# Transposes issued ahead of the loads two pairs on, and MoE pieces moved in front of the later first blocks, in an attention and feed-forward kernel

## The chip, the cores and the metric

The kernel runs on one core of one Trainium2 chip. The metric is the device time of one execution in microseconds (us). The engines of the core work side by side, each through its own queue of instructions in program order: PE (TensorE, matmuls), PEld (its weight loads), ACT (ScalarE), DVE (VectorE), POOL (GpSimd) and SP (SyncE, here only an issuer of DMAs).

## What is computed

Eight batches with eight heads each, 576 positions and head width 64. The attention has a decay: with `cum = cumsum(log(clip(f)))`, the scores are `q k^T / 8 + cum_i - cum_j`, masked to the causal half, softmaxed and multiplied by `v`. The heads of a position side by side make a row of 512 numbers, 4608 rows in all, and these go through a feed-forward layer, called MoE in the code:

```python
h = x @ w_in                          # 4608x512 by 512x2048
g = h * (1.0 / (1.0 + np.exp(-h)))
out = g @ w_out                       # 2048x512, float32
```

## The kernel before, in words

**The attention.** Each batch has a first block of 128 positions (all heads together, `turn0`, `scores0`, `out0`, `back0`) and the rest of its positions, done by pairs of heads: 4 pairs per batch, 32 pairs `n`. A pair takes this way. `load_qk(n)` (L144) issues four DMAs of 96 KB on SP for q and k in float32. `cast_qk(n)` (L371) has POOL write them as bf16 into a tile `qkb`, with a slice of a tails tile that `load_tails(b)` (L157) brings once per batch. `transposes(n)` (L400) is one DMA on SP, a DMA transpose from `qkb` into a tile `qkT` (L404). `scores(n, c)` (L425) for c = 0, 1, 2 multiplies on PE from `qkT` into PSUM, and ACT takes the exponential into `u`. `attend(n)` (L465) multiplies by the values, `back(m)` (L506) turns the results of two pairs and puts them into the rows `x` of the feed-forward layer.

**The buffers.** `qkT` has 3 buffers, which the first blocks use too, so that `transposes(n)` waits until `scores(n-3, 2)` has read the oldest; `qkb` has 4, the float32 stages 4, the output tiles `osb` 5. PSUM has two kinds: `psc`, 2 tiles for scores, and `pbig`, 4 tiles for all else (`hp`, `po`, `dn`, `tx`).

**The feed-forward layer.** The rows are cut into groups: group 0 is the first blocks of batches 0 to 3, group 1 those of 4 and 5, group 2 those of 6 and 7, then one group for the rest of each batch. A piece is either one `m1_chunk` (L528: four matmuls `hp`, then tanh on ACT and a product on DVE into `gt`) or one `m2_part` (L562: four matmuls `po` of width 512; after the fourth part of a tile ACT copies it to `osb`, and a store is kept in a list that SP issues later). A group's pieces can be placed only once it is in `ready`, and parts of the second product only once `open2` is set.

**The order.** It is written out by hand: every engine runs its instructions in the order in which the program emits them (L54). `fill(us)` (L641) emits pieces until their planned PE time, 4·(width/2.4 + 2.5) ns each, has used up `us` microseconds; it stops early if no piece can be placed. So the numbers in `fill` decide how many pieces stand at a place of the PE queue. `two_more(b, ...)` (L740) does the first blocks b and b+1 with small fills between; it stands twice, for 4 and 5, and for 6 and 7. After it comes the loop over m (L801), two pairs per pass: `scores`, `prepare(n)` (L772), a `slot` of pieces, and so on, with `attend` of both pairs at the end of a pass. `prepare(n)` issues what later pairs need: the loads of pair n+4, cast and transpose of pair n+2, tails and values of the next batch. `slot` also emits, after its pieces, the stores that were waiting before it.

Of the kernel before, what the change touches and what calls it, by code (L numbers as in the profile page):

```python
# [18 lines left out]
def kernel(  # L19
# [25 lines left out]
    NU = B * NP  # L45
# [95 lines left out]
    def head(p, i):  # L141
        return p // 2 * 4 + 2 * i + p % 2

    def load_qk(n):  # L144
        b, p = divmod(n, NP)
        ts = []
        for name, src in (("qf", q), ("kf", k)):
            t = stage.tile([P, NR, 2, D], FP32, name=name, tag=name, bufs=4)
            for i in range(2):
                nc.sync.dma_start(  # L150
                    out=t[:, :, i, :],
                    in_=src[b, head(p, i), P:SM, :].rearrange("(c p) d -> p c d", p=P),
                )
            ts.append(t)
        qst[n] = tuple(ts)

    def load_tails(b):  # L157
        t = stage.tile([P, H, D], FP32, name="qktf", tag="qktf", bufs=2)
        for i, src in enumerate((q, k)):
            nc.sync.dma_start(  # L160
                out=t[i * ST : (i + 1) * ST, :, :],
                in_=src[b, :, SM:S, :].rearrange("h s d -> s h d"),
            )
        tst[b] = t

    def load_v(b, c):
        if c == 0:
            vst[b] = []
        t = vfs[c]
        r = slice(0, P) if c < NR else slice(ST, P)  # L170
        nc.sync.dma_start(
            out=t[r, :, 0:D],
            in_=v[b, :, P + c * P : min(S, P + (c + 1) * P), :].rearrange("h p d -> p h d"),
        )
        vst[b].append(t)
# [195 lines left out]
    def cast_qk(n):  # L371
        b, p = divmod(n, NP)
        t2 = conv.tile([P, NX, 2 * D], BF16, name="qkb", tag="qkb")
        for i, t in enumerate(qst.pop(n)):
            c0 = i * (NR + 1)
            nc.gpsimd.tensor_copy(  # L376
                out=t2[:, c0 : c0 + NR, :].rearrange("p c x -> p (c x)"),
                in_=t[:, :, :, :].rearrange("p c h d -> p (c h d)"),
            )
        nc.gpsimd.tensor_copy(  # L380
            out=t2[:, NR, :].rearrange("s (i d) -> s i d", i=2),
            in_=tst[b].rearrange("s (u i w) d -> s u w i d", u=2, w=2)[:, p // 2, p % 2, :, :],
        )
        qbf[n] = t2

    def convert_v(b, c):
        vbf[b] = vps[b % 2]
        r = slice(0, P) if c < NR else slice(ST, P)
        n = r.stop - r.start
        nc.gpsimd.tensor_tensor(  # L390
            out=vbf[b][r, c, :, :],
            in0=vst[b][c][r, :, :],
            in1=w_bf[r, c + 1, b * H : (b + 1) * H, None].to_broadcast([n, H, D + 1]),
            op=ALU.mult,
        )
# [4 lines left out]
    def transposes(n):  # L400
        src = qbf.pop(n)
        t = qktp.tile([P, NX, P], BF16, name="qkT", tag="qkT")
        qkT[n] = t[:, :, :].rearrange("p x c -> p (x c)")
        nc.sync.dma_start_transpose(  # L404
            out=t[:, :, :], in_=src[:, :, :].rearrange("p x c -> p (x c)")
        )
# [200 lines left out]
    def step():  # L607

        a, c = at["m1"], at["m2"]
        can1 = a < len(M1) and M1[a][0] in ready  # L610
        g1 = M1[a][0] if a < len(M1) else NG
        g2 = M2[c][0] if c < len(M2) else NG
        if can1 and M1[a][1] == 0 and g1 > g2 + 1:
            can1 = False
        can2 = open2["w"] and c < len(M2) and g2 < g1
        if not can1 and not can2:
            return None
        if can1 and can2:
            f1 = M1[a][1] / NFC
            f2 = (c - sum(M2_OF[:g2])) / M2_OF[g2]  # L620
            want = 3 - at["last"] if abs(f1 - f2) < 0.15 else (1 if f1 < f2 else 2)
            if want == at["last"] and at["row"] >= 2 and abs(f1 - f2) < 0.25:
                want = 3 - want
            can1 = want == 1
        kind = 1 if can1 else 2
        at["row"] = at["row"] + 1 if kind == at["last"] else 1
        at["last"] = kind
        if can1:
            m1_chunk(*M1[a])
            at["m1"] += 1  # L630
            return 4 * (GW[g1] / 2.4 + 2.5)
        m2_part(*M2[c])
        at["m2"] += 1
        return 4 * (DM / 2.4 + 2.5)
# [6 lines left out]
    def fill(us_, first=0, least=0):  # L641
        if first:
            at["last"], at["row"] = 3 - first, 2
        at["left"] += us_ * 1000
        while at["left"] > 0 or least > 0:
            t = step()
            if t is None:
                at["left"] = 0.0
                return False
            at["left"] -= t  # L650
            least -= 1
        return True
# [76 lines left out]
    load_qk(2)  # L729
    load_v(0, 2)  # L730
    load_v(0, 3)
    for n in range(2):
        cast_qk(n)
        transposes(n)
    load_qk(3)
    load_tails(1)
    for c in range(NM):
        convert_v(0, c)
# [1 line left out]
    def two_more(b, banned):  # L740
        for x in range(2):
            turn0(b + x, 0)
            turn0(b + x, 1)
            fill(0.6, 0, 1)
        for x in range(2):
            if banned:
                scores0(b + x, ban0(b + x))
            else:
                scores0(b + x)
                mask0(b + x)  # L750
            fill(0.6 if x == 0 else 2.0, 2, 1 if x == 0 else 2)
        out0(b)
        fill(0.6, 0, 1)
        out0(b + 1)
        fill(0.8, 0, 2)
        back0(b, on_act)
        fill(0.6, 0, 1)
        back0(b + 1, on_act)
        fill(0.6, 2, 1)

    fill(4.0)
    two_more(4, True)
    ready.add(1)
    fill(6.0)
    open2["w"] = True
    fill(3.0, 2)
    two_more(6, False)
    ready.add(2)

# [2 lines left out]
    def prepare(n):  # L772

        b, p = divmod(n, NP)
        if n + 4 < NU:
            load_qk(n + 4)
        if n + 2 < NU:
            cast_qk(n + 2)
            transposes(n + 2)
        if p == 0 and b > 0 and b + 1 < B:  # L780
            load_tails(b + 1)
        if p == 1 and b + 1 < B:
            for c in range(NM):
                load_v(b + 1, c)
        if p >= 2 and b + 1 < B:
            for c in range(2 * (p - 2), 2 * (p - 1)):
                convert_v(b + 1, c)
# [13 lines left out]
    for m in range(NQ):  # L801
        n = 2 * m
        piece = 1.3 if m < 2 else 2.4
        scores(n, 0)
        scores(n, 1)
        prepare(n)
        slot(piece, 2)
        if m > 0:
            back(m - 1)
            if m % 2 == 0:  # L810
                b = m // 2 - 1
                pending.append([1, [REST_OF[b]] + ([TAILS_OF[b][0]] if b == NM - 1 else [])])
        scores(n, 2)
        scores(n + 1, 0)
        prepare(n + 1)
        slot(piece, 2)
        scores(n + 1, 1)
        scores(n + 1, 2)
        slot(piece, 2)
        attend(n)  # L820
        attend(n + 1)
        slot(min(3.5, max(0.8, behind() - LAG)) if m > 1 else 0.8, 1)
# [38 lines left out]
```

The softmax here doesn't subtract the row's maximum and nothing guards it: scores larger than these inputs give would overflow.

## Time and profile before

| | |
|---|---|
| time before, median of 13 runs | 360.06 us (358.74 to 362.7) |
| the profiled execution's own time | 359.35 us |
| its span in the profile | 357.6 us |
| PE busy | 342.6 us, 96% of the span |
| ACT busy | 219.3 us, 61% |
| DVE busy | 184.2 us, 52% |
| POOL busy | 103.1 us, 29% |
| moved by DMA | 47.92 MB, mean 134 GB/s |
| DMA transposes `qkT` on SP | 32, median 3.2 us from issue to landing |
| q and k loads on SP | 128 of 96 KB, medians 3.2 and 3.1 us to landing |

The profile is one execution. In a timeline, a row is a start, a length, an engine, a line of the kernel, the tiles (written <- read), a count, and in brackets the idle time before it and what ended that. In a list of waits a row names who waited for whom, the total, the number of times and the longest. The rows of a window view give the busy time of each engine in a stretch, then the clock that PE was granted (1.00 is full speed), the DMA share and rate. The time lies 1.75 us above the span, before and behind what the profile covers.

### The profile page before, as it was taken

What the parts mean: (1) busy time and instruction counts of PE and PEld (TensorE: products, weight loads), DVE (VectorE), ACT (ScalarE), POOL (GpSimd) and SP (SyncE); (2) the same over time, 40 slices, a digit from 0 to 9 for tenths busy, and PEclk for the clock granted to TensorE, in tenths of its full rate; (3) what the DMA queues carried; (4) which work ended last, traced back from release to release, by engine and by line L of the source; (5) the groups of instructions that cost most, each with busy time, mean ns of one, the idle gap of its engine ahead of it and who ended that gap; (6) DMA issues with size and microseconds to landing.
All of it is one profiled execution on the core that took longest, in us unless ns stands there. A gap on an engine that the chain in (4) does not pass through costs nothing.

```text
span 357.6 us, 9042 instructions
## 1 busy us (share of the span) xinstructions
PE 342.6 (96%) x3647; PEld 205.1 (57%) x3647; DVE 184.2 (52%) x408; ACT 219.3 (61%) x400; POOL 103.1 (29%) x183
## 2 busy tenths in 40 slices
PE   7999997779999999999999999999999999999995
PEld 3644554556756656656566565765656655555564
DVE  4565743435566655556554563456645553435340
ACT  5656646657586776866857567576776744444341
POOL 6975246263171351072072053116100000000000
PEclk9999999989999999999999999999999999999999
DMA  8999979899996966987596495498520001001012
GB/s 158 222 206 212 208 158 178 200 208 193 174 216 148 211 136 124 162 172 156 125 199 151 105 215 113 119 174 187 83 55 31 31 5 55 29 36 55 31 60 59
DMA packets 139001, 47.92 MB, mean 134 GB/s; under 512 B 128016, under 2 KB 134416, under 8 KB 138960
## 3 DMA queue, kind: packets, MB, share of 16 engines
q1 hardware_dynamic: 132272, 40.93, 55.8%
q0 software_dynamic: 6528, 6.29, 10.7%
q8 instruction: 28, 0.46, 0.6%
q10 hardware_dynamic: 160, 0.13, 0.1%
q14 instruction: 13, 0.11, 0.1%
HBM read 36.85 MB, written 9.44 MB: 129 GB/s over the span
## 4 chain that ended last, share of the span: by engine, by line
PE 75%; DMA 11%; SPq 5%; ACT 4%; issue 2%; POOL 1%; DVE 1%; ACTq 0%; POOLq 0%
PE po L580 32%; PE hp L535 28%; PE sc L436 6%; DMA vf<-in_v_dram 5%; PE dn L481 4%; DMA w_out_bf<-in_moe_w_out_dram 3%; SPq L150 3%; PE dn L490 2%; DMA qkT<-qkb 2%; ACT u L440 2%; PE tx L511 2%; DMA qkb<-in_q_dram 1%; SPq L160 1%; DVE gt L544 1%; ACT th L543 1%
## 5 line engine op out<-in xcount | busy, mean ns | idle before, releaser
L544 DVE SCALAR_TENSOR_TENSOR gt<-th,hp 128x384 bf16<-128x384 bf16 (+2 forms) x208 | 106.4, 522 | 83.7 <-ACT th L543 80.0
L580 PE MATMUL po<-w_out_bf,gt 128*128 128x512 bf16 (+1 forms) x592 | 147.7, 376 | 0.0
L543 ACT ACTIVATE th<-hp 128x384 bf16<-128x384 f32 (+2 forms) x208 | 96.0, 476 | 84.0 <-PE hp L535 79.1
L535 PE MATMUL hp<-x,w_in_bf 128*128 128x384 bf16 (+2 forms) x704 | 130.5, 322 | 1.1 <-DVE gt L544 0.8
L535 PEld LDWEIGHTS <-w_in_bf 128*128 128x128 bf16 x832 | 79.1, 98 | 56.5 <-issue 3.1
L440 ACT ACTIVATE u<-sc 128x1024 bf16<-128x1024 f32 (+1 forms) x96 | 74.5, 816 | 22.2 <-PE sc L436 22.0
L580 PEld LDWEIGHTS <-gt 128*128 128x128 bf16 x592 | 54.5, 98 | 48.8 <-issue 3.5
L390 POOL TENSOR_TENSOR vp<-vf,w_bf 128x520 bf16<-128x520 f32 (+1 forms) x32 | 34.3, 1074 | 58.0 <-DMA vf<-in_v_dram 41.7
L445 DVE TENSOR_TENSOR u<-u,tri 128x768 bf16<-128x768 bf16 x32 | 18.6, 582 | 30.8 <-ACT u L440 30.7
L436 PE MATMUL sc<-qkT 64*128 64x128 bf16 (+1 forms) x640 | 26.9, 208 | 5.3 <-DMA qkT<-qkb 4.6
L590 ACT ACTIVATE osb<-po 128x512 f32<-128x512 f32 (+1 forms) x37 | 22.0, 595 | 15.0 <-PE po L580 15.0
L376 POOL CAST qkb<-qf 128x384 bf16<-128x384 f32 x32 | 16.1, 504 | 46.5 <-DMA qf<-in_q_dram 46.0
L436 PEld LDWEIGHTS <-qkT 64*128 64x128 bf16 x640 | 18.4, 95 | 14.9 <-DMA qkT<-qkb 6.1
L459 DVE TENSOR_TENSOR ut<-ut,trit 128x128 bf16<-128x128 bf16 x32 | 9.2, 288 | 31.6 <-ACT ut L452 31.3
L452 ACT ACTIVATE ut<-sc 128x640 bf16<-128x640 f32 x32 | 22.9, 716 | 0.0
L481 PEld LDWEIGHTS <-u 128*128 128x128 bf16 x576 | 20.9, 97 | 3.3 <-issue 1.1
L481 PE MATMUL dn<-vp,u 128*128 128x65 bf16 x384 | 21.8, 193 | 0.0
L481 PE MATMUL dn<-v,u 128*128 128x65 bf16 x192 | 19.8, 193 | 0.9 <-DVE gt L544 0.8
L499 DVE TENSOR_TENSOR xr<-dn,rec 128x448 bf16<-128x448 f32 x32 | 20.0, 624 | 1.1
L376 POOL CAST qkb<-kf 128x384 bf16<-128x384 f32 x32 | 17.0, 533 | 9.7 <-DMA kf<-in_k_dram 9.6
L535 PE MATMUL hp<-xt,w_in_bf 128*128 128x256 bf16 x128 | 17.7, 273 | 0.0
L436 PE MATMUL sc<-qkT,kT 64*128 64x64 bf16 (+1 forms) x128 | 16.0, 258 | 0.0
(65 smaller groups left out, 202.3 us busy)
## 6 DMA issues: line engine op xcount, KB each, us to landing
vf<-in_v_dram SPq DMA_DIRECT2D x32, 256.0 KB, 4.8
out_dram<-osb SPq DMA_DIRECT2D x32, 256.0 KB, 2.2
qf<-in_q_dram SPq DMA_DIRECT2D x64, 96.0 KB, 3.2
kf<-in_k_dram SPq DMA_DIRECT2D x64, 96.0 KB, 3.1
w_in_bf<-in_moe_w_in_dram POOLq DMA_DIRECT2D x4, 512.0 KB, 8.9
w_out_bf<-in_moe_w_out_dram POOLq DMA_DIRECT2D x4, 512.0 KB, 11.0
qkb<-in_q_dram POOLq DMA_DIRECT2D x8, 128.0 KB, 5.9
qkb<-in_k_dram POOLq DMA_DIRECT2D x8, 128.0 KB, 6.6
```

The lines of the kernel that those rows point to most:

```text
L376: nc.gpsimd.tensor_copy(out=t2[:, c0 : c0 + NR, :].rearrange("p c x -> p (c x)"), in_=t[:, :, :, :].rearrange("p c h d -> p (c h d)"),)
L390: nc.gpsimd.tensor_tensor(out=vbf[b][r, c, :, :], in0=vst[b][c][r, :, :], in1=w_bf[r, c + 1, b * H : (b + 1) * H, None].to_broadcast([n, H ...
L436: nc.tensor.matmul(sc[:, i, o : o + q1 - q0], lhsT=kt, rhs=t[r, q0:q1], start=True, stop=True)
L440: nc.scalar.activation(out=u[:, :, c * SM : c * SM + w], in_=sc[:, :, 0:w], func=ACT.Exp, scale=scale)
L452: nc.scalar.activation(out=ut[:, :, 0:3:2, :].rearrange("p k i t -> p i k t"), in_=sc[:, :, T0 : T0 + (NM + 1) * ST].rearrange("p i (k t) ...
L481: nc.tensor.matmul(dn[:, i * NR + c - 1, :], lhsT=u[:, i, o : o + P], rhs=vals(kb, i), start=(kb == 0), stop=(kb == c),)
L499: nc.vector.tensor_tensor(out=xq[:, :, p % 2, :], in0=dn[:, :, 0:D], in1=rec[:, :, None].to_broadcast([P, NGR, D]), op=ALU.mult,)
L535: nc.tensor.matmul(hp[:, :], lhsT=w_in_bf[:, cc, fc * P : (fc + 1) * P], rhs=xg(g)[:, cc, :], start=(cc == 0), stop=(cc == NCC - 1),)
L543: nc.scalar.activation(out=th[:, :], in_=hp[:, :], func=ACT.Tanh, scale=0.5)
L544: nc.vector.scalar_tensor_tensor(out=gt[:, fc, :], in0=th[:, :], scalar=1.0, in1=hp[:, :], op0=ALU.add, op1=ALU.mult,)
L580: nc.tensor.matmul(po[:, :], lhsT=gt[:, fc, tb * P : (tb + 1) * P], rhs=w_out_bf[:, fc, m0:m1], start=(fc == 0), stop=(fc == NFC - 1),)
L590: nc.scalar.activation(out=osb[:, :], in_=po[:, :], func=ACT.Copy, scale=0.5)
```

## The change

Two kinds of edits. The DMA transposes are put ahead of loads in the order of SP: in `prepare`, the cast and transpose of pair n+2 now come before the loads of pair n+4, and in the run-up the loads of pair 3 come before the casts and transposes of pairs 0 and 1. And three arguments of `fill` change, in front of the first blocks 4 and 5 and of 6 and 7. The work itself is the same: no instruction is added or removed. POOL's order does not change.

```diff
     load_v(0, 3)
+    load_qk(3)
     for n in range(2):
         cast_qk(n)
         transposes(n)
-    load_qk(3)
     load_tails(1)
...
-    fill(4.0)
+    fill(6.0)
     two_more(4, True)
     ready.add(1)
-    fill(6.0)
+    fill(5.0)
     open2["w"] = True
-    fill(3.0, 2)
+    fill(6.0, 2)
     two_more(6, False)
     ready.add(2)
...
     def prepare(n):
 
         b, p = divmod(n, NP)
-        if n + 4 < NU:
-            load_qk(n + 4)
         if n + 2 < NU:
             cast_qk(n + 2)
             transposes(n + 2)
+        if n + 4 < NU:
+            load_qk(n + 4)
```

Compared instruction by instruction, the two PE queues hold the same 3647 matmuls. In front of `turn0(4)` stand seven `hp` pieces of width 512 instead of five. Between `two_more(4)` and `turn0(6)` stand twelve `hp` pieces of width 256 and seven `po` pieces, instead of two `hp` of 512, seven of 256 and three `po`. The pieces that are placed earlier are missing from the fills of later passes of the loop; from the last `back` on the two queues are alike again. On SP each transpose from pair 2 on stands ahead of one `load_qk` that it stood behind, and three stores instead of two stand ahead of the transpose of pair 3.

## The prediction

> **What bounds the kernel now.** I read the page's busy shares first, then the waits of PE, then PE's timeline around each wait, and last SP's timeline in the same stretch. PE is busy for 342.6 of 357.6 us, so the time can fall only where PE stands still or runs slowly. The list of PE's waits is short:
>
> ```profile
> PE sc L436 <- DMA qkT<-qkb: 4.6, 2, 3.1
> PE tp L271 <- DMA qkb<-in_q_dram: 1.7, 3, 1.0
> PE hp L535 <- DVE gt L544: 0.8, 1, 0.8
> PE dn L481 <- DVE gt L544: 0.8, 1, 0.8
> PE sc L436 <- ACT u L440: 0.5, 1, 0.5
> ```
>
> The timeline of PE places them (start, length, operation, count, idle before):
>
> ```profile
> 26.25 0.64 PE L271 MATMUL tp<-sel,qkb 128*64 128x64 bf16 x16 [0.31 <-DMA qkb<-in_q_dram]
> 27.13 0.64 PE L271 MATMUL tp<-sel,qkb 128*64 128x64 bf16 x16 [0.24 <-DMA qkb<-in_k_dram]
> ...
> 58.51 0.40 PE L436 MATMUL sc<-qkT 64*128 64x128 bf16 x8 [1.55 <-DMA qkT<-qkb]
> ...
> 72.81 0.61 PE L436 MATMUL sc<-qkT 64*128 64x128 bf16 x8 [3.07 <-DMA qkT<-qkb]
> 73.36 1.89 PE L580 MATMUL po<-w_out_bf,gt 128*128 128x512 bf16 x4
> ...
> 79.61 0.19 PE L481 MATMUL dn<-v,u 128*128 128x65 bf16 x1 [0.80 <-DVE gt L544]
> ```
>
> All lie before 100 us (the 0.85 us wait of `hp` for `gt` ends at 99.61); from 100 to 320 us PE idles 0.25 us in all, in the table of windows. So the run-up decides. The two waits for `qkT` are pair 0's first scores and pair 3's. Behind the second, four 512-wide `po` matmuls took 1.89 us where the ordinary four take 1.03. The windows view says why: in the third column from the end stands the granted clock.
>
> ```profile
> 69.74:72.81 3.07, 0.00 (x1) 0.00 (x0) 0.65 (x3) 1.02 (x3) 0.00 (x0) 0.94 0.57 111
> 72.81:76.00 3.19, 3.19 (x18) 1.43 (x20) 0.56 (x1) 1.62 (x2) 1.34 (x2) 0.53 1.27 234
> ```
>
> Why were the transposes late? SP issues without a pause from 37 to 105 us:
>
> ```profile
> 54.33 2.87 SPq L404 DMA_TRANSPOSE qkT<-qkb  x2
> 57.25 1.13 SPq L150 DMA_DIRECT2D qf<-in_q_dram  x2
> ...
> 64.14 1.25 SPq L404 DMA_TRANSPOSE qkT<-qkb  x1
> 65.43 1.06 SPq L559 DMA_DIRECT2D out_dram<-osb  x2
> 66.54 1.04 SPq L150 DMA_DIRECT2D qf<-in_q_dram  x2
> 67.62 1.15 SPq L150 DMA_DIRECT2D kf<-in_k_dram  x2
> 68.89 2.17 SPq L404 DMA_TRANSPOSE qkT<-qkb  x1
> ```
>
> Pair 3's transpose was issued at 68.89, right behind pair 5's loads, while POOL had finished its casts at 63.88. It landed at 72.77 (3.88 us in the chain), and PE began at 72.81. The wait is one for SP's order, not for data.
>
> **Part 1, pieces moved forward.** Their cost on PE, start to start in the timeline: 0.87 us for four matmuls of width 512, 0.435 for width 256. In front of blocks 4 and 5 stand two more 512-wide pieces, 1.73 us. That covers the two waits for `qkb` (0.31 + 0.24): gain 0.55. In front of 6 and 7: 5 more of 256 and 4 more `po`, less 2 `hp` of 512: 2.17 + 3.46 − 1.73 = 3.90 us. Together 5.63 us of work move ahead of pair 0. They are taken from later fills, so they cost nothing in sum while PE stays the bound; they shift pair 0, as well as the first blocks.
>
> A new wait comes with it. Group 0 has sixteen `hp` pieces, and seven in front of block 4 and nine inside `two_more(4)` now use them up; the fill behind the last `tx` of block 5, which in the old order found one more, finds none. So the next PE instruction is group 1's first `hp`, which reads the rows that ACT copies from that very `tx`. ACT first does the tanh of the last piece. In the trace of before the same ACT pair started 37.37 (tanh) and 37.86 (copy, 0.58 us, ending 38.44), and PE went on at 37.74. PE would now start at about 38.5: cost 0.75 (at least 0.6, one copy; at most 1.2, copy behind a whole tanh). Nothing covers it.
>
> Pair 0's scores are then due at 56.96 + 5.63 − 0.55 + 0.75 = 62.8, instead of 56.96.
>
> **Part 2, the order of SP.** Pair 3's loads (2.2 us of issue, 57.25 to 59.44) now come before transposes 0 and 1. These go out at about 56.5 instead of 54.33 and, with the 4.13 us to landing of before, pair 0's lands at 60.7, against 62.8: 2.1 us to spare, and the 1.55 us wait is gone. Pair 1's lands at about 62.1, wanted 2.4 us after pair 0's.
>
> For pair 3 I add SP's rows in the new order: transposes to 59.4, tails 2.2, transpose 2 1.25, loads of pair 4 2.2, three stores 1.6, so transpose 3 goes out at 66.7 and lands at 70.6. PE wanted it at 69.74, that is 11.2 after pair 0's start at 58.51; the fills between are 0.4 us shorter now, so it is due at 62.8 + 10.8 = 73.6. Three us to spare; the 3.07 wait goes, and with it the slow clock. The same sum for pair 4 (loads of pair 5 2.2, four value loads 3.2, a store 0.6): landing 77.9, due 79.8; for pair 5: 81.6, due 83.6. Later pairs have more, since even the old order had no wait after the fourth pair.
>
> What the slow clock cost: from 72.81 to 75.96 PE did a score group, a `po` and an `hp` piece. At full clock they take 0.24 + 0.87 + 0.44 = 1.55; they took 3.15. Gain 1.6. Here a rule of the Trainium skill disagrees with the row. "TensorE: Matmul & The Clock Gate", Part 1, has PE fall to half clock after at least one idle window of about 3.4 us. The gap was 3.07, so by the rule nothing is lost to the clock and the gain is 1.6 smaller. The row has 0.53 of the clock for 3.19 us; I take the row.
>
> **Part 3, runs of `hp` pieces.** The 0.80 and 0.85 us waits for `gt` come where three or five `hp` pieces in a row find ACT busy with exponentials (1.03 us each) and fill the four `pbig` tiles. In the new order the run of three before pair 3's `attend` has become one piece, and the run of five has become two: gain 1.65. But a run of four now stands before `attend(4)`, right behind scores whose exponentials take 1.03 + 0.39 + 0.70 on ACT: cost 0.9, between 0.8 (the rows of before) and 1.3. The short ACT wait of 0.54 at pair 1 stays.
>
> **The sum.** Gains 0.55 + 1.55 + 3.07 + 1.6 + 1.65 = 8.4. Costs 0.75 + 0.9, and 0.2 for small lateness of transposes: 1.85. Net 6.55 us. The profiled execution, 359.35 with a span of 357.6, would become 352.8 with 351.05. It lies 0.7 under the median of 360.06; from the median I get 353.5, rounded to 353.6. Costs at their ends: net 5.9 to 7.0. Since spares of two us hang on DMA landings that vary between 2.9 and 4.7 us, I let this case run from 352.4 to 355.4.
>
> **Rivals.** (a) Supply is still the bound, in part. For: the DMA share was 1.19 from 50 to 60 us and 1.23 from 75 to 85, and SP never rests; moving an issue does not make bytes flow faster, and faster PE wants pairs 4 and 5 earlier (due 2.1 and 1.6 us before their old times). Against: each transpose has 384 KB less in front of it, about 1.9 us at the 205 GB/s of those windows. If pair 0, 4 or 5 lands 3 to 5 us behind my sum, which spares about 2, then 1 to 3 us of wait come back, the longer ones with a part of the slow clock: 355 to 357.5, in the middle 356.
>
> (b) The wait only moves: the fills give up their pieces earlier, the passes of the loop that are now leaner stall for ACT by as much as was won. It takes 6.5 us of new waits, eight of the 0.8 us kind; only one such run is to be seen in the new order. About 360.
>
> (c) Slower. "DMA: Bandwidth & Descriptors", Anatomy of one DMA, says that a wait for a semaphore happens on the issuing sequencer before dispatch. So what stands behind a waiting transpose waits too, and the change puts the loads of pair n+4 there. The trace has the waits: SP's transposes waited for PE's scores (the buffer of pair n−1) 20.2 us in ten places, the longest 5.8. If all of that reached the loads and from them PE, the sum would be 20.2 − 6.5 = 13.7 slower, 374; half of it gives 10.1 − 6.5 = 3.6 slower, 363.7, which I take for this case; it is slower than before from a third on. By the rule alone I would expect such a loss. It decides only if the loads then come too late: load 3.2, casts 1.4, value conversion 2.2, transpose 4, some 11 us, against more than four pairs (a pass of two pairs takes about 14 us) between that wait and the pair's own scores, 28 us. So the wait is paid out of a reserve of 17 us. The same holds for stores behind it: five `osb` tiles, one filled every 5 us or so.
>
> **Chances.** My sum 0.68; (a) 0.20; (b), within 0.2% (0.7 us, about what a measurement of this kernel can tell from no change), 0.05; (c) 0.05; better than 352.4 0.02. Faster 0.90, same 0.04, slower 0.06. The range leaves out the last three and the end of (a): 352.2 to 357.2.
>
> **What would show it.** Right: no wait of `sc` for `qkT` in PE's list; clock 1.00 from 60 to 85 us; scores of pair 0 near 63, with PE without idle before them; a new gap near 0.75 between the last `tx` of block 5 and group 1's `hp`; one wait for `gt` near 0.9 before `attend(4)`; transposes issued near 56.5, 66.7 and 74. Wrong: a `qkT` wait at pair 0, 4 or 5 says (a); many new `gt` waits after 85 us say (b); casts on POOL that wait for loads behind SP's transposes, and `qkT` waits after 100 us, say (c).

## The result, and the profile after

The changed kernel takes 355.83 us in the median of 11 runs (354.41 to 357.21), the kernel before 360.03: a ratio of 0.988, 95% interval 0.9861 to 0.9899, some 4.2 us. The forecast was 353.6, and its range ran to 357.2. The gain is clear of the noise and about two thirds of what was forecast. The profiled execution has a span of 353.9 us instead of 357.6.

PE is busy for 342.4 us instead of 342.6; its idle time fell from 15.0 to 11.5 us. From the list of its waits (total, number, longest):

```profile
PE sc L436 <- DMA qkT<-qkb: 3.5, 2, 3.1
...
PE hp L535 <- ACT x L367: 0.8, 1, 0.8
```

The waits for `gt` are gone, the wait of `hp` for ACT's copy is new, and the wait for `qkT` is 3.5 us instead of 4.6. The timeline of PE shows where:

```profile
38.99 5.40 PE L535 MATMUL hp<-x,w_in_bf 128*128 128x256 bf16 x48 [0.78 <-ACT x L367]
...
61.80 0.40 PE L436 MATMUL sc<-qkT 64*128 64x128 bf16 x8
...
73.01 0.40 PE L436 MATMUL sc<-qkT 64*128 64x128 bf16 x8 [0.41 <-DMA qkT<-qkb]
...
82.42 0.40 PE L436 MATMUL sc<-qkT 64*128 64x128 bf16 x8 [3.09 <-DMA qkT<-qkb]
...
82.97 1.85 PE L580 MATMUL po<-w_out_bf,gt 128*128 128x512 bf16 x4
84.61 1.91 PE L535 MATMUL hp<-x,w_in_bf 128*128 128x256 bf16 x8
```

Pair 0 starts at 61.80 with no idle before it. Pair 3 (73.01) waits 0.41 instead of 3.07. But pair 4 now waits 3.09 (82.42), and the `po` and `hp` behind it take twice their usual time. In the kernel before, PE came to pair 4 without a wait:

```profile
81.87 0.40 PE L436 MATMUL sc<-qkT 64*128 64x128 bf16 x8
```

In the windows of the changed kernel (busy of PE, PEld, DVE, ACT and POOL, then granted clock, DMA share, GB/s) the clock is seen to fall, as it did behind pair 3 before:

```profile
79.33:82.42 3.09, 0.00 (x0) 0.00 (x1) 1.17 (x3) 0.38 (x1) 2.44 (x4) 1.00 1.23 136
82.42:85.56 3.14, 3.14 (x21) 1.60 (x22) 0.88 (x1) 1.94 (x2) 1.40 (x3) 0.60 1.22 195
```

So the large stall was not removed; it moved on to the next pair. Ahead of pair 4 PE has by then done 38 `hp` and 20 `po` pieces, instead of 33 and 17 before: about 4.8 us more, at the prediction's cost of a piece. SP's timeline shows how pair 4's transpose came to be late:

```profile
56.34 2.95 SPq L404 DMA_TRANSPOSE qkT<-qkb  x2
...
59.99 0.88 SPq L160 DMA_DIRECT2D qktf<-in_k_dram  x1
62.91 1.24 SPq L404 DMA_TRANSPOSE qkT<-qkb  x1
...
68.03 1.67 SPq L404 DMA_TRANSPOSE qkT<-qkb  x1
69.75 1.78 SPq L150 DMA_DIRECT2D qf<-in_q_dram  x2
71.57 1.02 SPq L150 DMA_DIRECT2D kf<-in_k_dram  x2
72.63 3.32 SPq L171 DMA_DIRECT2D vf<-in_v_dram  x4
76.06 0.55 SPq L559 DMA_DIRECT2D out_dram<-osb  x1
76.72 1.29 SPq L404 DMA_TRANSPOSE qkT<-qkb  x1
```

The last row is pair 4's. It landed at 82.37, 5.65 us after its issue (first row below, from the chain that ended last), with a pair's q and k loads, four value loads and a store in front of it. Before, it was issued at 77.60 (second row) and landed 3.9 us later, at 81.5.

```profile
76.72 5.65 DMA qkT<-qkb
```

```profile
77.60 1.25 SPq L404 DMA_TRANSPOSE qkT<-qkb  x1
```

So, although it now stands ahead of one pair's loads, it lands 0.9 us later. One cause is on POOL: the cast of pair 2 now waits for the landing of pair 0's transpose (5.21 us, behind the loads of pair 3), whose `qkb` buffer it writes over (beside the buffers of pairs 0 and 1, the other two of the four are those of the first blocks of batches 6 and 7). SP, whose next instruction is the transpose of pair 2, stands still from 60.87 to 62.91 for that cast.

```profile
61.70 0.50 POOL L376 CAST qkb<-qf 128x384 bf16<-128x384 f32 x1 [1.68 <-DMA qkT<-qkb]
```

In the kernel before this cast ran without a wait, as transpose 0 had landed at 58.46:

```profile
59.60 0.50 POOL L376 CAST qkb<-qf 128x384 bf16<-128x384 f32 x1
```

### The profile page after: what moved, and what is told of

Same layout as the page of the kernel before. It is cut to its first block, busy times and chain, and to the rows that moved or that the text cites. A ratio compares the mean times of both kernels' runs of the same rounds, so it can differ in the third digit from the quotient of the medians.

```text
span 353.9 us, 9037 instructions
## 1 busy us (share of the span) xinstructions
PE 342.4 (97%) x3647; PEld 205.3 (58%) x3647; DVE 185.8 (53%) x408; ACT 217.8 (62%) x400; POOL 103.5 (29%) x183
## 4 chain that ended last, share of the span: by engine, by line
PE 75%; DMA 13%; SPq 6%; POOL 3%; issue 2%; ACT 1%; DVE 0%; POOLq 0%
PE po L580 31%; PE hp L535 29%; PE sc L436 6%; PE dn L481 4%; DMA vf<-in_v_dram 4%; SPq L150 4%; DMA w_out_bf<-in_moe_w_out_dram 4%; DMA qkT<-qkb 3%; PE dn L490 2%; PE tx L511 2%; DMA qkb<-in_k_dram 1%; SPq L160 1%; DMA kf<-in_k_dram 1%; POOL qkb L124 1%; POOL v L326 1%
## 5 line engine op out<-in xcount | busy, mean ns | idle before, releaser
L543 ACT ACTIVATE th<-hp 128x384 bf16<-128x384 f32 (+2 forms) x208 | 95.5, 477 | 82.3 <-PE hp L535 79.8
L445 DVE TENSOR_TENSOR u<-u,tri 128x768 bf16<-128x768 bf16 x32 | 21.6, 675 | 26.6 <-ACT u L440 26.6
L459 DVE TENSOR_TENSOR ut<-ut,trit 128x128 bf16<-128x128 bf16 x32 | 7.8, 245 | 29.5 <-ACT ut L452 29.4
```

What stands on the lines that cost most here:

```text
L445: nc.vector.tensor_tensor(out=x, in0=x, in1=tri[:, None, None, :].to_broadcast([P, 2, NR, P]), op=ALU.mult,)
L543: nc.scalar.activation(out=th[:, :], in_=hp[:, :], func=ACT.Tanh, scale=0.5)
```

## The experiments

The intervals are those of the ratio to the kernel before, measured beside each run. After the result, the theory (A) was that the landing of pair 4's transpose sets the time as long as PE comes to it early.

**Each part alone.** The first two runs undo one part each.

```diff
# e1_order_only: the changed kernel with the old fills
-    fill(6.0)
+    fill(4.0)
     two_more(4, True)
     ready.add(1)
-    fill(5.0)
+    fill(6.0)
     open2["w"] = True
-    fill(6.0, 2)
+    fill(3.0, 2)
# e2_fills_only: the kernel before with fills of 6.0, 5.0 and 6.0
```

> Only the order on SP is changed, the fills are as before. Theory A (the transposes' landings are a supply line, and the time is the landing of pair 4's transpose, 82.4 in the changed kernel, plus the PE work left then): pair 0 waits some 4.6 us for its transpose (landing 61.5 against 57.0), pair 4's lands near 82.4 as in the changed kernel, and 5.6 us of pieces that the fills had moved forward are still to do, less the 0.8 us wait that the fills bring: 360 to 361 us, no gain. Theory B (the order on SP is what removed pair 3's wait and made the gain): 356 to 357 us, pair 3's wait gone.

Measured: 358.38 us, ratio 0.9962 (0.9946 to 0.9978), in neither theory's range. The order alone gains a little. It removes the wait of pair 3 and brings none at pair 4, and pays for it at pair 0 (here PE's timeline and then a window of the same run):

```profile
60.98 0.61 PE L436 MATMUL sc<-qkT 64*128 64x128 bf16 x8 [3.72 <-DMA qkT<-qkb]
```

```profile
64.00:65.00 1.00, 1.00 (x21) 0.61 (x18) 0.00 (x0) 0.63 (x2) 0.00 (x0) 0.50 1.11 37
```

Pair 0's wait grew from 1.55 to 3.72 us, and the clock stood at 0.50 from 61 to 66 us. Theory A had pair 4's transpose land at 82.4; here it was issued at 76.42 and landed 3.9 us later, at 80.3. So the landing is not a fixed point: it is another one in each version.

> Only the fills are changed, the order on SP is as before. Theory A: transposes land as in the kernel before (pair 0 58.5, pair 3 72.8, pair 4 81.5), pair 4 is due near 79.5, so it waits about 2 us with less loss of clock than in the changed kernel: 354 to 355.5 us. Theory B: the gain is gone, 359 to 360 us, pair 3 waits as before. Theory C (the new order made pair 4 late through pair 2's cast, and the old order would have none of it): no wait for a transpose above 0.5 us, 351.5 to 352.5 us.

Measured: 356.24 us, ratio 0.9908 (0.9892 to 0.9924), again in no theory's range; A, the nearest, had about 2 us of wait at pair 4. Most of the gain comes from the fills: the changed kernel's own interval overlaps this one, if barely. Pair 3 waits less, pair 4 as long as in the changed kernel:

```profile
73.32 0.40 PE L436 MATMUL sc<-qkT 64*128 64x128 bf16 x8 [0.85 <-DMA qkT<-qkb]
82.75 0.40 PE L436 MATMUL sc<-qkT 64*128 64x128 bf16 x8 [3.11 <-DMA qkT<-qkb]
```

Theory C, that the new order alone made pair 4 late, falls: in the old order pair 4 waits 3.11. The fills bring PE to pair 4 at 79.64, 2.2 us sooner than before, and its transpose (issued at 78.05, 4.7 us to landing) lands at 82.7, 1.2 us later than before.

**More work ahead of pair 4.**

```diff
# e3_piece_m1 and e3_again, from the changed kernel
-        piece = 1.3 if m < 2 else 2.4
+        piece = 1.3 if m < 1 else 2.4
```

> The changed kernel with three larger slots in the second pass of the loop (2.4 instead of 1.3 us), so that about 3.3 us of pieces more lie ahead of pair 4. Theory A: pair 4 is due near 82.6, its transpose lands at 82.4: wait below 0.5 us, no half clock behind it, gain 3.1 + 1.6 us: 351 to 351.7 us. Rival (the wait only moves on, each later pair is as late): pair 5 or 6 waits about 2 to 3 us, 354 to 356 us.

Measured: 351.92 us, ratio 0.9784 (0.9765 to 0.9802), a little above theory A's range. As it has it, pair 4 waits 0.19, and the clock stays at 1.00; but the transpose landed at 83.7, not at 82.4.

```profile
83.76 0.40 PE L436 MATMUL sc<-qkT 64*128 64x128 bf16 x8 [0.19 <-DMA qkT<-qkb]
...
90.69 1.02 PE L580 MATMUL po<-w_out_bf,gt 128*128 128x512 bf16 x4 [0.84 <-DVE gt L544]
```

The second row is a wait behind a run of four `hp` pieces. It is a cost of the larger slots: the run stands between the scores of pair 5, not in front of `attend(4)`, where the prediction had one for 0.9.

> The changed kernel with larger slots in the second pass, again, for a comparison on one chip. Theory A: 3.5 to 4.5 us under the changed kernel of this call.

Measured beside the changed kernel on one chip: 351.92 us, ratio 0.9774 (0.9745 to 0.9803).

> The changed kernel itself, on the chip of the other runs of this call, as the mark that they are measured against: 355 to 356.5 us, a wait of about 3 us for pair 4's transpose.

Measured: 356.0 us, ratio 0.9884 (0.9859 to 0.991), a wait of 2.72 at pair 4. Three larger slots are thus worth 4.1 us, about the wait and the slow clock behind it.

**The values out of the way.**

```diff
# e4_values_later, from the changed kernel
-        if p == 1 and b + 1 < B:
+        if p == 2 and b + 1 < B:
             for c in range(NM):
                 load_v(b + 1, c)
-        if p >= 2 and b + 1 < B:
-            for c in range(2 * (p - 2), 2 * (p - 1)):
+        if p == 3 and b + 1 < B:
+            for c in range(NM):
                 convert_v(b + 1, c)
```

> The changed kernel with the value loads of the next batch issued behind the transpose of the pair after, and their conversions one prepare later. If the 0.9 MB of values in front of pair 4's transpose make it late: it is issued near 73.5 and lands near 77.5, no wait at pair 4; pair 5's transpose is then behind the values, lands near 84 and may wait 1 us: 352 to 353 us. If its lateness comes from SP's rows in sum whatever their order: the same wait of about 3 us, 355 to 356.5 us.

Measured: 355.14 us, ratio 0.9879 (0.9859 to 0.99). In SP's timeline pair 4's transpose stands ahead of the values and pair 5's behind them:

```profile
74.70 1.28 SPq L404 DMA_TRANSPOSE qkT<-qkb  x1
...
78.64 3.78 SPq L171 DMA_DIRECT2D vf<-in_v_dram  x4
82.54 1.91 SPq L404 DMA_TRANSPOSE qkT<-qkb  x1
```

Pair 4's landed 3.5 us after its issue and PE did not wait for it. Pair 5's made PE wait, and the clock fell again (PE's timeline, then a window):

```profile
86.67 0.40 PE L436 MATMUL sc<-qkT 64*128 64x128 bf16 x8 [1.78 <-DMA qkT<-qkb]
```

```profile
87.67:88.67 1.00, 1.00 (x4) 0.30 (x3) 0.50 (x1) 0.74 (x2) 1.00 (x3) 0.50 0.94 316
```

So the values delay the transpose behind them by their own 3.3 to 3.8 us of issue, and moving them hands the wait to the pair behind them. That they also lengthen the way to landing (3.5 here against 5.65) is not shown: pair 5's transpose, right behind them, landed after 4.1 us. In the run with the order alone the same value loads and store stand in front of pair 4's, and it landed after 3.9:

```profile
71.13 4.46 SPq L171 DMA_DIRECT2D vf<-in_v_dram  x4
75.72 0.58 SPq L559 DMA_DIRECT2D out_dram<-osb  x1
76.42 1.29 SPq L404 DMA_TRANSPOSE qkT<-qkb  x1
```

The long way is not chance, as it was 5.6, 5.5 and 5.6 us in the other traces of the changed kernel and of `e3`; its cause stays open.

**The run-up put back.**

```diff
# e9_runup_old, from the changed kernel
-    load_qk(3)
     for n in range(2):
         cast_qk(n)
         transposes(n)
+    load_qk(3)
```

> The changed kernel with only the run-up put back: the loads of pair 3 behind the transposes of pairs 0 and 1, as before; in the loop the transposes stay ahead. In the changed kernel transpose 0 landed at 61.55 behind those loads, and POOL's cast of pair 2 waited for it until 61.7. If this is what makes pair 4 late: transpose 0 lands near 58.5, the cast of pair 2 ends near 61.2, transposes 2 to 4 go out some 1.3 us sooner, and pair 4 waits 1.3 to 2.3 us instead of 3.1: 353.5 to 355 us. If not: pair 4 waits 2.7 to 3.4 us as before, 355 to 356.5 us.

Measured: 354.57 us in the median, ratio 0.9821 (0.9778 to 0.9864), but the six runs are of two kinds: 351.02 and 351.60 with a mean clock of 1.000, and 354.40 to 355.25 with 0.993 to 0.995. The median lies in the first theory's range, but the one trace does not have its wait of 1.3 to 2.3 us at pair 4. The profile is one of the first kind (SP's row of pair 4's transpose, then PE's of pair 4):

```profile
75.24 1.29 SPq L404 DMA_TRANSPOSE qkT<-qkb  x1
```

```profile
79.40 0.40 PE L436 MATMUL sc<-qkT 64*128 64x128 bf16 x8 [0.27 <-DMA qkT<-qkb]
```

The transposes of pairs 2, 3 and 4 went out at 61.49, 66.60 and 75.24, by 1.4 to 1.5 us sooner than in the changed kernel, as the theory had it, and pair 4's landed after 4.1 us instead of 5.65, behind the same value loads. It landed 3.0 us sooner in all, so in this trace the run-up edit is the larger part of pair 4's lateness. In this form the kernel stands at the edge: in some runs pair 4 hardly waits, while the clock of the others fits a wait like that of the changed kernel. Only the first kind has a trace. It also settles what a run of four `hp` pieces costs in front of `attend(4)`:

```profile
87.25 2.07 PE L535 MATMUL hp<-x,w_in_bf 128*128 128x256 bf16 x16
89.46 0.19 PE L481 MATMUL dn<-v,u 128*128 128x65 bf16 x1
```

From the start of the run to `attend` it is 2.21 us, the same as in the changed kernel (91.95 to 94.16), where the stall stood in front; four pieces at 0.435 are 1.74.

**The small waits, and the order once there is cover.**

```diff
# e5_pieces_old_order: the kernel before with fills of 6.0, 5.0 and 6.0,
#   and piece = 1.3 if m < 1 else 2.4
# e6_keep_piece, from e3_piece_m1
-    fill(6.0)
+    fill(5.0)
     two_more(4, True)
...
-    fill(5.0)
+    fill(7.6)
     open2["w"] = True
# e7_keep_piece_more and e7_again: as e6, with 7.0 and fill(7.0, 2)
# e8_more_old_order: the pieces of e7, order on SP as before
```

> The fills of the change and the larger slots of the second pass, with the order on SP as before the change. If the order on SP is worth nothing once pieces cover pair 4: the time of the run with the new order and the same pieces, 351.7 to 352.7 us, a wait for pair 4's transpose of 0 to 1 us (it landed at 82.7 in the run with the fills alone, due 83.6). If the order still shortens the supply: pair 4 or 5 waits over 1.5 us, 353.5 to 355 us.

Measured: 352.35 us, ratio 0.9761 (0.9728 to 0.9794). Five executions took 351.97 to 352.67; the one that was traced took 695.81, for a reason that stays open, so its trace says nothing on pair 4. By the ratio the time is that of the new order with the same pieces (0.9784 and 0.9774).

> The larger slots, and one piece of group 0 kept behind the last tx of block 5, the same pieces in sum ahead of pair 4. The 0.8 us wait of hp for ACT's copy goes. Theory A (the landing of pair 4's transpose is the bound whenever PE is early): pair 4 is due 0.8 us sooner, near 82.8, and waits 0.8 to 1 us for its transpose, without a loss of clock: the same 351.9, from 351.5 to 352.3. Rival (each PE wait is worth its own length): 351.1 us, and no more than 0.3 us at pair 4.

Measured: 352.42 us, ratio 0.9767 (0.9736 to 0.9799). The 0.8 us wait for ACT's copy is gone, and no wait at pair 4 above 0.2 has come, where theory A had 0.8 to 1; yet the time is not better. Waits of 0.2 to 0.6 us stand in its place, for `qkb` in block 4 and for DVE at `out0` of blocks 6 and 7.

> As the run before it, with 1.4 us more pieces ahead of pair 4. Theory A: pair 4 is due near 84.2 and does not wait; with both waits gone 0.8 us under the run with the larger slots: 350.9 to 351.4. Rival (pieces spent early bring waits for gt of the same size later): 351.7 to 352.5, waits for gt above 1.5 us in sum between 85 and 110.

Measured: 352.5 us, ratio 0.9769 (0.9736 to 0.9803). The time is the rival's, but not by its waits for `gt`: between 85 and 110 us the list has none.

> The version with one piece kept behind the last tx and more pieces ahead of pair 4, again. Theory A (waits for transposes gone in both, one 0.8 us wait for ACT's copy gone here): 0.3 to 1 us under the run with the larger slots of this call. Rival (ACT waits of the same size come in its place, as its first profile with 1.4 us of waits for u makes one expect): within 0.3 us of it.

Measured: 352.81 us, ratio 0.9793 (0.9767 to 0.9818), against 351.92 beside it for the version with the larger slots alone. It is not faster than that. Theory A's 0.8 us is not there; a wait for ACT's exponentials has come where more pieces had stood between the scores of pairs 0 and 1:

```profile
65.50 0.23 PE L436 MATMUL sc<-qkT 64*128 64x128 bf16 x2 [0.90 <-ACT u L440]
```

> The same pieces as the run before it, with the order on SP as before the change, so that only four numbers of the fills differ from the kernel before. If the order on SP is worth nothing under cover: within 0.5 us of the run before it, 350.9 to 351.9. If it is worth something: pair 4 or 5 waits over 1 us for its transpose, 352.5 to 354.

Measured: 352.83 us, ratio 0.9777 (0.9746 to 0.9807), beside 352.5 for the new order. With more pieces ahead of pair 4, the order of SP makes no difference that these runs can tell.

The version that is best in all its runs is `e3`, 351.92 both times. The old run-up together with the larger slots was not tried.

## Why the prediction was right, and where it was not

The sign and the range held; the time came out where rival (a) had it (355 to 357.5), to which 0.20 was given. The main case, 352.4 to 355.4, did not come: that the range held is owed to the rival, not to the sum.

**Part 1 held.** The waits for `qkb` at 26 and 27 us are gone. The new wait of `hp` for ACT's copy was set at 0.75 and measured 0.78. Pair 0 was due at 62.8 by the sum and started at 61.80, without a wait; but its transpose had landed only at 61.55, so the spare was 0.25 us and not 2.1. That most of the gain is in the fills is shown by the run with the fills alone.

**Part 2 failed** in the sentence "landing 77.9, due 79.8" for pair 4. The due time was nearly right, 79.33. The landing was 82.37, 4.5 us late, in three terms. Transpose 2 was set to go out at 61.6 and went at 62.91, as its cast on POOL waited for transpose 0; the prediction counted the buffers of `qkT` but not those of `qkb`. Another 1.4 us of issue was added by transpose 3 (1.67 instead of 1.25) and the rows behind it, pair 5's loads most of all, 2.84 us where 2.2 was assumed. And the way to landing was taken as 3.9 us, while it took 5.65, for a reason that the runs leave open. Against 1.9 us of reserve and 0.5 of due time that makes the 3.09 us wait, and behind it the half clock. The `po` and the two `hp` pieces behind it cost 3.35 us instead of 1.74, about 1.6 more, as in the kernel before. So 3.1 + 1.6 + 0.4 for pair 3 came off the forecast gain; `e3` gives back 4.1 of it by more pieces alone.

The prediction also took the edit in the run-up for harmless, since pair 0 had 2.1 us to spare. Nearly all of that was used up, POOL waited behind it, and in the run with the order alone nothing covered it: 3.72 us.

**Part 3 held for the gain**: both waits for `gt` are gone. The cost of 0.9 for the run of four `hp` pieces was set too high. It is some 0.5 (2.21 us instead of 1.74), with the stall at pair 4 in the changed kernel and without it in the run with the old run-up, so the stall did not hide it.

**Rivals.** (a) is what happened: PE came to pair 4 2.5 us sooner than before, and the transpose landed no sooner, in the new order as in the old one with the new fills. SP's and POOL's order have a part in it, as the run with the old run-up shows; how much the bytes in flight have is not separated. (The windows that it names have 209 and 211 GB/s, not 205, which changes nothing in it.) (b) did not happen: there is no wait for `gt` after 85 us. (c) did not happen either, as was argued. From 100 us on, SP's transposes wait more for PE with the new order than the 20.2 us of before,

```profile
SPq L404 <- PE sc L436: 32.3, 12, 4.8
```

and the loads behind them wait with them, yet PE has no wait for `qkT` there, which fits the reserve of some 17 us.

The sum does not close. Of the forecast 6.55 us, 5.1 fell away, and 1.1 came on top: 0.4 and 0.2 of costs that were set too high, and 0.44 by which the changed kernel is ahead at 18 us already (the last `tx` row there starts at 18.29 instead of 18.73), through the landing of the first loads. That makes 2.5 us; the two spans are 3.7 apart, and the other 1.2 are not resolved.

## What to carry to other kernels

Work moved ahead of a late transfer is worth its length only until the next transfer on the same queue is late: make the sum of issue and landing for several transfers on, with a range for the landing (here 2.9 to 6.3 us) and not one figure. When an issue is moved, follow its buffer on every engine that writes it again. And ask of every stall of 2 or 3 us on PE what clock it leaves behind; in the traces here that was half its price again.

## What was not expected of the hardware

A gap of 1.78 us on PE (`e4`) was followed by 3.4 us at half clock, as were gaps of 2.72 to 3.11, and the gap of 3.72 (`e1`) brought 6.8 us, twice as much; in the windows the half clock began 2.2 to 4.2 us after PE had stopped. Gaps of 0.85 (`e2`, at pair 3) and 1.55 (before, at pair 0) left the clock at 1.00. "TensorE: Matmul & The Clock Gate", Part 1, of the Trainium skill speaks of at least one idle window of about 3.4 us; in these runs much less was enough. In the traces the matmuls then take twice as long. What that costs in the time of a run is less clear. Of twelve executions of the changed kernel whose clock is listed, two had a mean of 0.998 and 1.000 and took 354.41 and 354.89 us, the others, at 0.993 to 0.995, 355.39 to 357.21. But of the 33 executions of the kernel before that were measured beside the runs, the eleven at 0.998 to 1.000 have a median of 360.5, and the sixteen at 0.993 to 0.995 one of 359.6: without the half clock they were no faster, and none of them was traced.

A DMA transpose took from 2.9 to 6.3 us from issue to landing; rows of the same kind in front of it (four value loads and a store) gave 3.9, 4.1 and 5.65.
